# The third chunk's q and k by seven block products, and the gate's logits as two more columns of v

## The chip, the cores and the metric

One core of one Trainium2 chip runs the whole kernel. The metric is device time in microseconds (us): the median of the runs, here 413.5 us over three runs (413.33 to 413.57).

## The reference, cut to what matters

```python
# x: [1, 2048, 448]; 16 heads of 28; window W = 8, dilation 2; F = 1792
g = sigmoid((x * gate_w).sum(-1, keepdims=True))      # one logit per token
qkv = x @ wqkv                                        # [2048, 448] @ [448, 1344]
# attention: each token looks at itself and 7 earlier tokens, 2 apart
logits = einsum("bhsd,bhswd->bhsw", q, kg) * scale    # masked, softmax
a = einsum("bhsw,bhswd->bhsd", attn, vg) ... @ wo
h = relu(x @ w1 + b1); b = (h * h) @ w2 + b2
return g * a + (1 - g) * b
```

All is float32, and the kernel keeps that accuracy with a faster matmul type: each operand is split into a high part (rounded to the type `fp32r`) and a low part (what is left), and a product is the sum of three: high by high, high by low, low by high.

## The kernel before, in words

**Tiles and stages.** The 2048 tokens are four chunks of 512 (`CH`), each four tiles of 128. The contraction over 448 is three full tiles of 128 rows and one of 64. TensorE is used as two halves of 64 rows: two products of 64 rows run side by side, one on the low and one on the high rows, each into its own PSUM bank ("a pair"). A bank that has been added to from one half must not be added to from the other before the first half's work has ended. The kernel sees to that with a *turn*: a one-element memset on VectorE into the bank (`turn`, L196), which TensorE's next product into that bank has to wait for. The written order puts other pairs between a turn and the product that needs it.

Phase A goes through chunks 0, 1, 2 and 3 and computes q, k and v: chunk 0 in `qkv_first`, the others in two calls of `qkv_two`, 63 pairs each (`run`, `side_by_side`). Results go from PSUM to a stage tile by ScalarE (`qkv_evacuate`, L205) and to DRAM (`q_d`, `k_d`, `v_d`, L211). Raw tiles are loaded into a pool of two buffers (`raw_tile`); ScalarE casts the high part (L115), VectorE subtracts for the low part (L116, `split_full`). In chunk 3 a w1 piece's row also goes through one PSUM bank: ScalarE casts and copies it (L514, L515), and VectorE subtracts from the copy (L520, `split_copied`). The bank holds one row at a time.

The gate's logits are worked out on VectorE from the raw x (`z_product`, `z_sums`, L680 to L687), stored to `z_d`, loaded in another layout, and summed (`z_last`).

Phase B is the MLP over the four chunks, with the output products of the attention put between. The attention's own products run on GpSimd (L335, L342), their sums on VectorE (L336, L350). GpSimd begins when the first loads of q, k and v (L306, L307, L312) have come in.

**What sets the order.** Nothing is reordered: each engine runs its instructions as written, and so does SyncE, which issues all DMAs. The writing is driven by a clock of the kernel's own: each pair adds 203 ns (`MM448`) to it in `advance`, and work is put on a list with a due time (`when(time, ...)`, `at(delay, ...)`, `soon` is 1.5 us later). Whenever `advance` is called, all that is due is written in order of its due time, and after it the attention's next pieces; `flush` writes the VectorE reduce of a piece two pieces later. So an operation that is written before a turn stands before it on its engine, whatever it waits for. The table of due times is at L750 to L776, the loop over the chunks at L793 to L806. At the end of chunk 1 the attention is switched on, and its first three loads are written there.

Of the kernel before, what the change touches and what calls it, by code (L numbers as in the profile page):

```python
# [14 lines left out]
P = 128  # L15
# [8 lines left out]
NQ = D + 2  # L24
NZ = 64
NP = 512
# [31 lines left out]
def gated_mix_kernel(ctx: ExitStack, tc: tile.TileContext, xT, wqkv, w1, w2, wo, b1, b2, out):  # L58
# [11 lines left out]
    z_d = tc.dram_tile([P, NZ], F32, name="z_d")  # L70
# [10 lines left out]
    w1h = const.tile([P, 3, F], F32R, name="w1h")  # L81
    w1l = const.tile([P, 3, F], F32R, name="w1l")
# [8 lines left out]

    xpool = ctx.enter_context(tc.tile_pool(name="xpool", bufs=1))
# [5 lines left out]
    zg = smallp.tile([P, 6, NS], F32, name="zg")  # L98
    zt, gt, g1t = zg[:, 0:2], zg[:, 2:4], zg[:, 4:6]
# [54 lines left out]
    wqh = ap.tile([P, 3, NP + 2 * D], F32R, name="wqh")  # L154
    wql = ap.tile([P, 3, NP + 2 * D], F32R, name="wql")

    w7h = ap.tile([P, NP + D], F32R, name="w7h")
    w7l = ap.tile([P, NP + D], F32R, name="w7l")
# [3 lines left out]
    nc.gpsimd.memset(halo0, 0.0)  # L162

    stage = {}

    def block(b):

        o = (0, NP, NP + D)[b]
        return slice(o, o + D)
# [29 lines left out]
    def qkv_evacuate(pt, c, tl, b):  # L199
        par, t = c // 2, (c % 2) * 4 + tl  # L200
        first = (b, t // 2) not in stage
        if first:
            stage[b, t // 2] = xap.tile([P, G, 2, C], F32, tag="stage", name=f"st{c}_{tl}_{b}", bufs=ST_BUFS)
        st = stage[b, t // 2]
        nc.scalar.activation(st[:, :, t % 2], pt[:, :D].rearrange("p (g c) -> p g c", g=G), AF.Copy)  # L205
        if not first:
            stage.pop((b, t // 2))
            t0 = t - t % 2
            dst, off = ((q_d, 0), (k_d, HALO), (v_d, HALO))[b]
            dd = dst[par, :, off:off + SP].rearrange("g (p s) c -> p g s c", s=NS)[:, :, t0:t0 + 2]  # L210
            nc.sync.dma_start(dd.rearrange("p g s c -> p g (s c)"), st.rearrange("p g s c -> p g (s c)"))  # L211
# [9 lines left out]
    def last(x, acc, tl, b):  # L221

        sl = slice(tl * P, tl * P + P)
        n = block(1) if b == 2 else slice(0, D)
        h, l = w7h[:, n], w7l[:, n]
        return [(acc, x.x7[:, sl], h), (acc, x.x7[:, sl], l), (acc, x.x8[:, sl], h)]

    def accs(c, b, tls, tags):
        return [Acc(t, f"qkv{c}_{tl}_{b}", D) for t, tl in zip(tags, tls)]
# [60 lines left out]


# [101 lines left out]
    def gates(par):  # L393

        e = smp.tile([P, 32], F32, tag="e", name=f"e{par}")[:, :NS]
        nc.scalar.activation(e, zt[:, par], AF.Exp, scale=-1.0)
# [127 lines left out]
    def w1_piece(i, dt, gap):  # L524
# [4 lines left out]
        sl = slice(i * n, (i + 1) * n)  # L529

        def part(k):
            if k < 3 and i > 1:
                split_copied(dt + k * gap, raw[:, k, :n], [(slice(0, P), slice(0, n), w1h[:, k, sl], w1l[:, k, sl])])
                return
            if k < 3:
                split_full(raw[:, k, :n], w1h[:, k, sl], w1l[:, k, sl], soon)
# [48 lines left out]
    def h_full(x, acc, f, ks):  # L585
        fs = slice(f * P, f * P + P)
        return sum((three(acc, w1h[:, k, fs], w1l[:, k, fs], x.h[k], x.l[k]) for k in ks), [])
# [11 lines left out]
    def h_turn(accs, f):  # L599
        touch(w1h[:, 2].rearrange("p (f n) -> p f n", n=P)[:, f:f + 2, 0:1])  # L600
# [36 lines left out]
    raws = [raw_tile("wqraw0")]  # L637
    rx = raw_tile("xraw0")
    for k in range(4):
        if k < 3:  # L640
            nc.sync.dma_start(raws[0][:, k, :NQ], wqkv[0, :, k])
        else:
            for b, rows in ((0, slice(0, 64)), (1, slice(64, P))):
                nc.sync.dma_start(raws[0][rows, k, :NQ], wqkv[b, rows, k])
# [3 lines left out]
    for b, tag in ((1, "k"), (2, "v")):  # L648
        raw = attp.tile([P, 3, D], F32, tag=tag, name=f"wqraw{b}")
        for k in range(3):  # L650
            nc.sync.dma_start(raw[:, k], wqkv[b, :, k, :D])
        raws.append(raw)
    raw7 = attp.tile([P, D], F32, tag="q", name="wqraw7")
    nc.sync.dma_start(raw7, wqkv[2, :, 3, :D])
    x = x_tiles(0, xap)
    for k in range(3):
        nc.scalar.activation(wqh[:, k, :D], raws[0][:, k, :D], AF.Copy)
# [7 lines left out]
        nc.vector.tensor_sub(wql[:, k, :D], raws[0][:, k, :D], f32(wqh[:, k, :D]))  # L665
        for cols in halves:
            nc.vector.tensor_sub(x.l[k][:, cols], rx[:, k, cols], f32(x.h[k][:, cols]))
    split_full(raws[0][:, 3, :D], w7h[:, :D], w7l[:, :D])
    split_x78(rx[:, 3], x.x7, x.x8)

    zs = smp.tile([P, 3, NZ], F32, tag="lg", name="zs")
    zu = xcp.tile([P, CH], F32, tag="zu", name="zu")
    zpart, zall, gw = zs[:, 0], zs[:, 1], zs[:, 2, 0:4]
    nc.vector.tensor_copy(gw, raws[0][:, :, D])

    def z_product(raw, k):

        r = slice(0, P if k < 3 else 64)
        if k:
            nc.vector.scalar_tensor_tensor(zu[r], raw[r, k], gw[r, k:k + 1], zu[r], op0=ALU.mult, op1=ALU.add)  # L680
        else:
            nc.vector.tensor_scalar_mul(zu, raw[:, 0], gw[:, 0:1])

    def z_sums(c):

        nc.vector.transpose(zu, zu)
        nc.vector.tensor_reduce(  # L687
            zpart.rearrange("p (b c t) -> p c t b", b=4, c=4)[:, c],
            zu.rearrange("p (t b r) -> p t b r", t=4, b=4), axis=AX.X, op=ALU.add)

    def z_store():

        nc.sync.dma_start(z_d, zpart)

    def z_load():

        for b in range(4):
            nc.sync.dma_start(
# [522 lines left out]
```

## Time and profile before

| | |
|---|---|
| median of three runs | 413.5 us (413.33 to 413.57) |
| span of the profiled execution | 412.0 us |
| TensorE busy | 407.8 us, 99% |
| VectorE / ScalarE / GpSimd busy | 270.6 / 210.4 / 268.4 us |
| granted TensorE clock | 1.000 |
| DMA moved | 73.83 MB, mean 179 GB/s |

The page gives for the profiled execution only its span, from the first to the last instruction; the runs' times hold what lies around it as well. In a line of the timeline the columns are: start, duration, engine, line, operation, what it writes and reads, shape, how many were merged, and in brackets the idle time before it with what ended it. A line of the waits reads: who waited for whom, us in total, how many times, the longest. A line of the DMA issues reads: what was moved, how many times, KB each, median us from issue to landing.

### The profile page before, as it was taken

How to read it: one execution, taken by the hardware profiler on the slowest of the kernel's cores; microseconds unless marked ns; L12 is line 12 of the kernel's file. 1: busy time of each engine (PE TensorE's matmuls, PEld its weight loads, DVE VectorE, ACT ScalarE, POOL GpSimd, SP SyncE). 2: the span in 40 equal slices, each digit the busy share in tenths (PEclk: the TensorE clock that was granted, in tenths of full speed). 3: DMA queues.
4: the chain of work that ended last, by engine and by line, in shares of the span. 5: the costliest groups of instructions: out<-in, count | busy, mean ns of one | idle time of the engine just before them, and what ended most of it. 6: DMA issues, size and time to landing. Idle time of an engine off the chain costs nothing.

```text
span 412.0 us, 9331 instructions
## 1 busy us (share of the span) xinstructions
PE 407.8 (99%) x3835; PEld 366.0 (89%) x3835; DVE 270.6 (66%) x430; ACT 210.4 (51%) x461; POOL 268.4 (65%) x167
## 2 busy tenths in 40 slices
PE   8999999999999999999999999999999999999997
PEld 7999999999888888888888888989898888888996
DVE  4590745276767766787656798879576677892354
ACT  4641646387775555444565535444653254346540
POOL 0000001955999999989989899999899977940000
PEclk9999999999999999999999999999999999999999
DMA  7999999979262315654112649765146530168304
GB/s 213 368 351 309 286 390 288 355 223 315 91 241 99 128 51 209 208 186 152 41 47 105 222 158 270 196 146 154 28 157 200 217 130 2 45 179 132 95 0 181
DMA packets 66763, 73.83 MB, mean 179 GB/s; under 512 B 33120, under 2 KB 59296, under 8 KB 66464
## 3 DMA queue, kind: packets, MB, share of 16 engines
q1 hardware_dynamic: 66720, 73.23, 55.4%
q8 instruction: 30, 0.49, 0.5%
q14 instruction: 13, 0.11, 0.1%
HBM read 45.74 MB, written 28.28 MB: 180 GB/s over the span
## 4 chain that ended last, share of the span: by engine, by line
PE 99%; DVE 0%; issue 0%
PE b L186 33%; PE h L186 32%; PE qkv L186 23%; PE a L186 7%; PE qkv L255 2%; PE warm L634 1%; PE a L993 1%; PE last L993 0%; DVE bt L872 0%; PE last L985 0%; PE a L985 0%; DVE zero L631 0%; DVE b1z L632 0%
## 5 line engine op out<-in xcount | busy, mean ns | idle before, releaser
L335 POOL TENSOR_TENSOR qk<-q,k 128x896 f32<-128x896 f32 x64 | 135.2, 2144 | 84.2 <-DMA k<-k_d 76.0
L342 POOL TENSOR_TENSOR av<-lg,v 128x896 f32<-128x896 f32 x64 | 119.2, 1957 | 6.2 <-DVE lg L336 5.6
L621 DVE TENSOR_TENSOR h<-h,h 128x512 fp32r<-128x512 f32 x56 | 38.4, 688 | 66.8 <-ACT h L624 66.5
L186 PE MATMUL qkv<-wqh,x 64*128 64x448 f32 x528 | 78.2, 359 | 0.0
L336 DVE TENSOR_REDUCE lg<-qk 128x32 f32<-128x896 f32 x64 | 67.0, 1074 | 0.0
L350 DVE TENSOR_REDUCE o<-av 128x112 f32<-128x896 f32 x64 | 66.4, 1070 | 0.1
L186 PE MATMUL b<-w2ah,h 64*128 64x448 f32 x448 | 66.3, 359 | 0.0
L186 PE MATMUL b<-w2bh,h 64*128 64x448 f32 x448 | 66.1, 359 | 0.0
L622 ACT ACTIVATE h<-h,b1z 128x512 f32<-128x512 f32 x56 | 36.7, 655 | 43.6 <-PE h L186 43.6
L186 PEld LDWEIGHTS qkv<-wqh,x 64*128 64x128 f32 x528 | 49.4, 184 | 3.6
L186 PE MATMUL qkv<-wql,x 64*128 64x448 f32 x264 | 47.7, 358 | 0.0
L186 PEld LDWEIGHTS b<-w2bh,h 64*128 64x128 f32 x448 | 42.1, 184 | 3.5
L186 PEld LDWEIGHTS b<-w2ah,h 64*128 64x128 f32 x448 | 42.0, 184 | 3.7
L205 ACT ACTIVATE st<-qkv 128x448 f32<-128x448 f32 x48 | 23.5, 542 | 34.3 <-PE qkv L186 31.7
L186 PE MATMUL b<-w2bl,h 64*128 64x448 f32 x224 | 40.7, 358 | 0.0
L186 PE MATMUL b<-w2al,h 64*128 64x448 f32 x224 | 40.5, 358 | 0.0
L623 ACT ACTIVATE h<-h 128x512 fp32r<-128x512 f32 x56 | 33.5, 598 | 1.7
L624 ACT ACTIVATE h<-h 128x512 f32<-128x512 f32 x56 | 33.3, 594 | 0.0
L573 ACT ACTIVATE h<-h 128x4 fp32r<-128x4 f32 (+1 forms) x35 | 7.2, 207 | 44.4 <-PE b L186 44.2
L186 PE MATMUL h<-x2b,w1h 64*128 64x512 f32 x168 | 28.1, 386 | 0.0
L186 PE MATMUL h<-x,w1h 64*128 64x512 f32 x168 | 28.1, 386 | 0.0
L186 PE MATMUL h<-x1b,w1h 64*128 64x512 f32 x168 | 28.1, 386 | 0.0
(150 smaller groups left out, 688.6 us busy)
## 6 DMA issues: line engine op xcount, KB each, us to landing
k<-k_d SPq DMA_DIRECT2D x8, 840.0 KB, 5.6
v<-v_d SPq DMA_DIRECT2D x8, 840.0 KB, 5.0
x_d<-x SPq DMA_DIRECT2D x11, 512.0 KB, 6.8
q_d<-st SPq DMA_DIRECT2D x8, 448.0 KB, 5.5
k_d<-st SPq DMA_DIRECT2D x8, 448.0 KB, 5.2
v_d<-st SPq DMA_DIRECT2D x8, 448.0 KB, 5.8
w1raw<-w SPq DMA_DIRECT2D x4, 896.0 KB, 9.2
q<-q_d SPq DMA_DIRECT2D x8, 448.0 KB, 3.6
```

The lines of the kernel that those rows point to most:

```text
L186: nc.tensor.matmul(acc.pt[:, :acc.n], a[rows], w[rows], start=acc.todo == acc.all, stop=acc.todo == 1)
L205: nc.scalar.activation(st[:, :, t % 2], pt[:, :D].rearrange("p (g c) -> p g c", g=G), AF.Copy)
L255: nc.tensor.matmul(acc.pt[:, :D], a, w, start=k == j == 0, stop=False)
L335: nc.gpsimd.tensor_mul(pr, q[:, s:s + 1].to_broadcast([P, W, C]), k[:, s:s + W])
L336: pending.append(lambda: nc.vector.tensor_reduce(lg[:, s], pr.rearrange("p w (h d) -> p w h d", h=HG), axis=AX.X, op=ALU.add))
L342: nc.gpsimd.tensor_mul(pr.rearrange("p (h d) w -> p w h d", h=HG), lg[:, s][:, :, :, None].to_broadcast([P, W, HG, DH]), v[:, s:s + W].rea ...
L350: nc.vector.tensor_reduce(o[:, g * C:(g + 1) * C], pr, axis=AX.X, op=ALU.add)
L573: nc.scalar.activation(ap, f32(ap), AF.Copy)
L621: nc.vector.tensor_sub(hl, pt, f32(hh))
L622: ops += [lambda pt=pt, r=r: nc.scalar.activation(pt, pt, AF.Relu, bias=b1t[:, f + r:f + r + 1]), lambda pt=pt, hh=hh: nc.scalar.activatio ...
L623: lambda pt=pt, hh=hh: nc.scalar.activation(hh, pt, AF.Square),
L624: lambda pt=pt, r=r, low=low: (nc.scalar.activation(pt, pt, AF.Square), at(delays[r], low))]
```

## The change

**q and k of chunk 2** are no longer computed tile by tile. Two groups (tiles 0 and 1; tiles 2 and 3) each take q and k of their two tiles as a 2 by 2 block product, cut into halves of the contraction, by seven products of sums instead of eight (Strassen's way). A half is a full tile of 128 and 64 rows more; what is left of the contraction (64 rows) is added in the plain way. For this, sums of weights (`wsum`) are made on VectorE in chunks 0 and 1, in place in the raw weights, and sums of tokens (`sums`) at the end of chunk 1, in place in the raw x of chunk 2. All four sums of `token_sums` are VectorE additions; each result is split into high and low. v of the chunk is written between the products.

A bank takes several of the seven products in turn: its content is copied to a stage tile on ScalarE (`copied`) or added to it on VectorE (`added`), and the next product is added on in the bank.

**The gate's logits** become two more columns of v's weights, 450 instead of 448, in all chunks. ScalarE copies the logit column out of the bank. The code on VectorE and the way through `z_d` go.

**Buffers.** The second half of w1 (`w1b`, six tiles) lies in a pool `halfp` of tags e0 to e5. Before w1 gets there, e0 to e3 hold first the raw q weights and then the token sums, and e4 the k stage of the second group. The raw q weights no longer take a raw buffer. x of chunk 1 has its fourth tile elsewhere, and chunk 3's copies of x (`x_copies`) are made in chunk 3 instead of chunk 2. The stage tiles of v in chunk 2 come from the pool of the attention's products.

**Due times.** Chunk 3's raw x is loaded at 47.5 us of the clock instead of 39.5, the second w1 piece at 54.0 instead of 46.5 with its first cast at 60.5 instead of 58.5; the later pieces are due 1.0 to 2.0 us sooner.

The diff, cut to its core:

```diff
+    def w1_second():
+        for n in range(2):
+            for k in range(3):
+                w1b[n][k] = halfp.tile([P, FA], F32R, tag=f"e{3 * n + k}", name=f"w1b{'hl'[n]}{k}")
...
-    def qkv_evacuate(pt, c, tl, b):
+    def qkv_evacuate(pt, c, tl, b, inner=False):
...
+        nc.scalar.activation(st[:, :, t % 2], heads(pt), AF.Copy)
+        if b == 2:
+            nc.scalar.activation(zt[par][:, t:t + 1], pt[:, D:D + 1], AF.Copy)
...
+    def beside(low, high):
+        assert len(low[1]) == len(high[1])
+        for a in range(0, len(low[1]), 3):
+            for i in range(a, a + 3):
+                for bank, prods in (low, high):
+                    bank.add(*prods[i])
+            advance(3 * MM448)
+
+    def turned(*banks):
+        for bank in banks:
+            nc.vector.memset(bank.pt[0:1, 511:512], 0.0)
...
+    class Group:
...
+        def first(self, n):
+            return self.to(n), sum((passes(*(tuple(v[self.rows] for v in o) for o in self.operands(n, half)))
+                                    for half in (False, True)), [])
+        def second(self, n):
+            return self.to(n), passes(*(tuple(v[self.others] for v in o) for o in self.operands(n, False)))
+        def rest(self, n, r, b):
+            a, w = self.tokens(r, 2), weights(b, 2)
+            return self.to(n), passes(*(tuple(v[self.others] for v in o) for o in (a, w)))
+        def to(self, n):
+            name = {1: "x", 2: "y", 3: "z", 4: "w", 5: "z", 6: "x", 7: "x"}[n]
...
+        def stage(self, b):
+            if self.st[b] is None:
+                if b == self.u == 1:
+                    t = halfp.tile([P, FA], F32, tag="e4", name=f"st{self.c}_{self.u}_{b}")
...
+        def copied(self, n, b, r):
+            nc.scalar.activation(self.stage(b)[:, :, r], heads(self.to(n).pt), AF.Copy)
+        def added(self, n, b, r, store=False):
+            st = self.stage(b)
+            nc.vector.tensor_add(st[:, :, r], heads(self.to(n).pt), st[:, :, r])
+            if store:
+                stage_store(st, self.c // 2, (self.c % 2) * 4 + 2 * self.u, b)
+
+    def qkv_seven(c, x, inner):
+        two = [Group(c, u, x) for u in range(2)]
...
+        v = V(c, x, (0, 1), inner)
+        v.first()
+        first(1)
+        v.second()
+        first(2)
+        second(1)
+        each("copied", 1, 0, 0)
+        first(5)
+        second(2)
+        other(2, 0, 0)
+        each("added", 2, 0, 0)
+        second(5)
+        each("copied", 5, 1, 1)
+        first(6)
+        first(4)
+        second(6)
+        each("copied", 6, 1, 0)
+        other(3, 0, 1)
+        second(3, True)
+        second(4)
+        first(7)
+        other(4, 1, 0)
+        v = V(c, x, (2, 3), inner)
+        v.first()
+        second(7)
+        each("copied", 7, 0, 1)
+        each("added", 4, 0, 1, True)
+        first(3, False)
+        each("added", 3, 1, 0)
+        v.second()
+        other(7, 1, 1)
+        each("added", 7, 1, 1, True)
...
     def h_turn(accs, f):
-        touch(w1h[:, 2].rearrange("p (f n) -> p f n", n=P)[:, f:f + 2, 0:1])
+        if f == NFA - 1:
+            for r in range(2):
+                touch(w1_f(0, 2, f + r)[:, 0:1])
+        else:
+            half = w1_rows(0, 2)[f // NFA].rearrange("p (f n) -> p f n", n=P)
+            touch(half[:, f % NFA:f % NFA + 2, 0:1])
...
+    def weight_sums():
+        (q0, q1, q2, m), (k0, k1, k2) = ([t[:, :D] for t in raws[b]] for b in range(2))
+        o = raw7[:, 1, :D]
+        sub = nc.vector.tensor_sub
+        def cut(key, t):
+            return lambda: split_full(t, *wsum[key], soon)
+        def by_halves(low, high):
+            return [lambda: low(LOW), lambda: high(HIGH)]
+        return [lambda: split_full(o, *w7x, soon),
+                lambda: sub(q0, k0, q0), lambda: sub(k0, k1, k0), cut((1, False), q0),
+                lambda: sub(k1, k1, q0), cut((3, False), k0), lambda: sub(q1, q1, k1),
+                cut((2, False), k1), cut((4, False), q1),
+                lambda: sub(q2, k2, q2),
+                *by_halves(lambda r: sub(k2[r], o[r], k2[r]), lambda r: sub(k2[r], m[r], k2[r])),
+                cut((1, True), q2), cut((3, True), k2),
+                *by_halves(lambda r: sub(o[r], o[r], q2[r]), lambda r: sub(m[r], m[r], q2[r])),
+                *by_halves(lambda r: sub(m[r], m[r], o[r]), lambda r: sub(o[r], o[r], m[r])),
+                *by_halves(lambda r: split_full(o[r], *(t[r] for t in wsum[2, True]), soon),
+                           lambda r: split_full(m[r], *(t[r] for t in wsum[2, True]), soon)),
+                *by_halves(lambda r: split_full(m[r], *(t[r] for t in wsum[4, True]), soon),
+                           lambda r: split_full(o[r], *(t[r] for t in wsum[4, True]), soon))]
+
+    def token_sums(c):
...
+        def cut(j):
+            split_full(xraw[c][:, j], *(t[:, :CH] for t in sums[c, j]), soon)
+            for u, rows in enumerate((LOW, HIGH)):
+                split_full(xraw[c][rows, 2 + j, u * 2 * P:(u + 1) * 2 * P], *(t[rows, CH:] for t in sums[c, j]), soon)
+        return [lambda: add(r(two, 1), r(two, 1), r(one, 1)), lambda: sub(r(one, 1), r(one, 0), r(one, 1)),
+                lambda: sub(r(one, 0), r(two, 1), r(one, 0)), lambda: sub(r(two, 0), r(two, 0), r(one, 0)),
+                lambda: (begin(), cut(1)), lambda: cut(0)]
...
-        xm[c] = x_tiles(c, xpool)
-        xs[c] = X(own + xm[c].t[3:])
-        for j in range(3):
-            at(12000.0 + j * 2000.0, lambda j=j: nc.scalar.activation(xm[c].t[j], f32(own[j]), AF.Copy))
+        xs[c] = X(own + [xpool.tile([P, 2, CH], F32R, tag="x3", name=f"x{c}_3")])
+
+    def x_copies(c):
+        own = xs[c].t
+        xm[c] = X([xpool.tile([P, 2, CH], F32R, tag=f"x{j}", name=f"x{c}_{j}") for j in range(3)] + own[3:])
+        for j in range(3):
+            at(3000.0 + j * 2000.0, lambda j=j: nc.scalar.activation(xm[c].t[j], f32(own[j]), AF.Copy))
...
-    SPLIT_AT = {1: 19000.0, 2: 35000.0, 3: 53500.0}
+    SPLIT_AT = {1: 19000.0, 2: 35000.0, 3: 55000.0}
...
+    steps(17000.0, 900.0, weight_sums())
...
-            when(t + 4500.0, x_more, c + 1)
...
+    when(23500.0, x_more, 2)
+    when(47500.0, x_more, 3)
+    when(46900.0, lambda: steps(47000.0, 900.0, token_sums(2)))
...
-    when(46500.0, w1_piece, 1, 58500.0, 1500.0)
-    when(67000.0, w1_piece, 2, 77400.0, 1450.0)
-    when(68000.0, w1_piece, 3, 83300.0, 1450.0)
-    when(70000.0, biases)
-    when(86000.0, w2_piece, 0, 4, 93000.0, 1400.0)
-    when(89600.0, w2_piece, 4, 3, 100200.0, 1400.0)
+    when(54000.0, w1_piece, 1, 60500.0, 1500.0)
+    when(66000.0, w1_piece, 2, 75600.0, 1450.0)
+    when(67500.0, w1_piece, 3, 81500.0, 1450.0)
+    when(68000.0, biases)
+    when(84000.0, w2_piece, 0, 4, 91200.0, 1400.0)
+    when(87600.0, w2_piece, 4, 3, 98400.0, 1400.0)
...
+    qkv_first(xs[0])
+    qkv_two(xs[1], 1, 0)
+    qkv_two(xs[1], 1, 2)
+    st_["spilled"] = 0
+    clock["on"] = True
+    clock["att"] = clock["pe"] - 1.0
+    advance(0.0)
+    qkv_seven(2, xs[2], True)
+    x_copies(3)
+    x = xs[3]
+    qkv_two(x, 3, 0, copies=True)
+    qkv_two(x, 3, 2, (mlp_one, mlp_two), True)
+    st_["spilled"] = 1
```

More of the change, by code (lines that the diff above doesn't have):

```diff
@@ L228, in accs @@
     def accs(c, b, tls, tags):
[L229 removed]
+        return [Acc(t, f"qkv{c}_{tl}_{b}", NV if b == 2 else D) for t, tl in zip(tags, tls)]
     def run(c, todo, steps):
@@ L585, in h_full @@
     def h_full(x, acc, f, ks):
-        fs = slice(f * P, f * P + P)
-        return sum((three(acc, w1h[:, k, fs], w1l[:, k, fs], x.h[k], x.l[k]) for k in ks), [])
+        return sum((three(acc, w1_f(0, k, f), w1_f(1, k, f), x.h[k], x.l[k]) for k in ks), [])
     def h_last(x, acc, f):
@@ L722, in x_begin, with steps @@
+    def steps(t, gap, fns):
+        for i, fn in enumerate(fns):
+            when(t + i * gap, fn)
     def x_begin(c):
```

240 lines of the change are left out of this document (151 added, 89 removed).

## The prediction

> **What bounds the kernel now.** I read the page first, then TensorE's row of the timeline, then SyncE's, ScalarE's and VectorE's rows between 46 and 93 us, then the waits.
>
> ```profile
> span 412.0 us, 9331 instructions
> PE 407.8 (99%) x3835; PEld 366.0 (89%) x3835; DVE 270.6 (66%) x430; ACT 210.4 (51%) x461; POOL 268.4 (65%) x167
> ...
> PE 99%; DVE 0%; issue 0%
> ```
>
> TensorE is busy for 407.8 of 412.0 us and is the whole chain that ended last. So a matmul taken out is time gained, and a wait that TensorE has not got today is time lost; no other engine gives any of it back. The span stands 1.5 us under the median of 413.5 us; I sum on the median.
>
> ```profile
> 52.66 0.56 PE L186 MATMUL qkv<-wqh,x 64*128 64x448 f32 x4
> ...
> 56.26 0.56 PE L186 MATMUL qkv<-wqh,x 64*128 64x448 f32 x4
> ...
> 104.60 0.40 PE L186 MATMUL h<-x,w17h 64*128 64x512 f32 x2
> ...
> 107.37 0.36 PE L186 MATMUL qkv<-wqh,x 64*128 64x448 f32 x2
> ```
>
> These are starts. 52.66 to 56.26 holds 18 pairs of 64-row products, 0.200 us a pair of 448 columns; the twelve pairs of 512 columns of the MLP's first visit take 104.60 to 107.37, 0.231 us each, so a column is 0.5 ns. The pair at 56.26 is the last of chunk 1, and chunk 2 begins at 56.46. The kernel's own clock (203 ns a pair) says 51.16 there, since 252 pairs lie behind it; that lets me turn its due times into places among the pairs.
>
> **The gain.** q and k of a chunk are 4 x 2 x 21 = 168 products, 84 pairs. In the new order each of two groups has seven times 6 + 3 products and four times 3, 75 in all, beside the other group: 75 pairs. Nine pairs are gone: 9 x 0.200 = 1.80 us. The gate's two columns ride on 168 pairs of v: 168 x 2 x 0.5 ns = 0.17 us. **Net -1.63 us.** The Z work (16 multiply-adds, 4 transposes, 4 sums) leaves VectorE, and 22 steps of weight sums come to it in about the same stretch, chunks 0 and 1; at 0.6 to 0.7 us a step they replace what goes (rows below), so I take nothing for them, with a bound of 0.5 us if a turn there is late.
>
> **What is queued behind what.** A turn is a memset on VectorE that TensorE must wait for before the other rows may add into a bank. VectorE runs it in written order, behind everything written ahead.
>
> ```profile
> 46.95 0.34 SPq L567 DMA_DIRECT2D xraw<-xT  x1
> 47.34 2.63 SPq L142 DMA_DIRECT2D x_d<-x  x4
> ...
> 52.49 0.59 SPq L528 DMA_DIRECT2D w1raw<-w  x1
> 55.43 0.38 SPq L211 DMA_DIRECT2D q_d<-st  x1
> 55.91 0.47 SPq L211 DMA_DIRECT2D k_d<-st  x1
> 57.72 0.85 SPq L211 DMA_DIRECT2D v_d<-st  x1
> 63.16 0.33 SPq L306 DMA_DIRECT2D q<-q_d  x1
> 64.51 0.34 SPq L307 DMA_DIRECT2D k<-k_d  x1
> 65.85 0.32 SPq L312 DMA_DIRECT2D v<-v_d  x1
> ```
>
> ```profile
> SPq L306 <- DMA q_d<-st: 4.5, 1, 4.5
> ```
>
> ```profile
> 56.71 0.98 ACT L205 ACTIVATE st<-qkv 128x448 f32<-128x448 f32 x2 [0.87 <-ACT st L205]
> 57.72 2.19 ACT L115 ACTIVATE x<-xraw 128x512 fp32r<-128x512 f32 x4
> 61.87 1.05 ACT L115 ACTIVATE w1h<-w1raw 128x448 fp32r<-128x448 f32 x2 [1.96 <-DMA w1raw<-w]
> 70.48 2.95 ACT L736 ACTIVATE x<-x 128x1024 fp32r<-128x1024 f32 x3
> ```
>
> ```profile
> k<-k_d SPq DMA_DIRECT2D x8, 840.0 KB, 5.6
> v<-v_d SPq DMA_DIRECT2D x8, 840.0 KB, 5.0
> ...
> q_d<-st SPq DMA_DIRECT2D x8, 448.0 KB, 5.5
> k_d<-st SPq DMA_DIRECT2D x8, 448.0 KB, 5.2
> ...
> w1raw<-w SPq DMA_DIRECT2D x4, 896.0 KB, 9.2
> ```
>
> ```profile
> DMA to landing us min/median/max: 6.4/9.2/9.7
> ```
>
> SyncE stands still until chunk 1's stores land (4.5 us for q), then issues the attention's three loads at 63.16, 64.51 and 65.85, one per landed store: 1.3 us for 448 KB in queue order, 345 KB/us. The second w1 piece, issued at 52.49, came in at 61.87, when ScalarE had waited 1.96 us for it; the last row is the landing of such pieces, 6.4 to 9.7 us.
>
> **First loss: that w1 piece.** It moves from 46.5 to 54.0 on the clock, so from ahead of the attention's loads (written at 51.16) to behind them. With its 896 KB out of the way the stores land 896/345 = 2.6 us sooner, v's at 63.2 instead of 65.85; only then can SyncE issue v's load and, at about 63.5, w1. Ahead of it lie 448 + 840 + 840 KB of loads: by queue order 63.2 + (448 + 840 + 840 + 896)/345 = 72.0; by the shortest and longest landing 69.9 and 73.2. I take **71.5**, near queue order, as transfers overlap at the seams. Its first cast is due at 60.5, after pair 48 of chunk 2; the low part, 1.5 later, is written after pair 57, just ahead of the turn of bank x after product 6. TensorE needs that turn for pair 64, at 56.46 + 63 x 0.2 + 0.4 (next part) = 69.5. It gets it at landing + cast 0.6 + subtract 0.6 + memset 0.1 = landing + 1.3 = 72.8: **3.3 us** lost (1.7 to 5.0). Today the same cast waits too, but the turns lie elsewhere and the wait is hidden.
>
> **The short turns** earlier in chunk 2. Between v's first part and its second lie only 6 pairs, 1.2 us, and ScalarE still has the token sums to cast: 0.1. Between product 2's parts lie 15 pairs' worth from v's end, 3.0 us, in which v's two copies (0.98), two gate columns, x3's last two casts (2.19 for four, so 1.1), the subtract (0.69) and the memset must pass, 3.3 in all: 0.3. Together **0.4**, bounds 0 and 1.0. The next chunk's raw x, now loaded at 53 rather than 46.95, comes behind the spill and ahead of the stores, at about 59; ScalarE gets to its first cast at 59 to 60 (the copies that end at 57.7 today, and 1.3 us of casts for each of two token sums, worked out from the four casts in 2.19), and anything up to 61 hides behind the wait for v.
>
> ```profile
> 58.38 0.69 DVE L116 TENSOR_TENSOR x<-xraw,x 128x512 fp32r<-128x512 f32 x1 [5.91 <-DMA v_d<-halo]
> ...
> 83.83 0.62 DVE L520 TENSOR_TENSOR w1l<-copy,w1h 128x448 fp32r<-128x448 f32 x1 [5.06 <-ACT copy L515]
> ...
> 87.13 1.08 DVE L336 TENSOR_REDUCE lg<-qk 128x32 f32<-128x896 f32 x1
> 88.20 0.06 DVE L196 MEMSET qkv<- 1x1 f32 x2
> 88.32 1.13 DVE L520 TENSOR_TENSOR w17l<-copy,w17h 64x128 fp32r<-64x128 f32 x4
> 89.37 1.07 DVE L336 TENSOR_REDUCE lg<-qk 128x32 f32<-128x896 f32 x1
> 90.38 0.64 DVE L520 TENSOR_TENSOR w1l<-copy,w1h 128x448 fp32r<-128x448 f32 x1
> 90.44 0.06 DVE L196 MEMSET qkv<- 1x1 f32 x2
> ```
>
> ```profile
> 86.58 1.22 ACT L514 ACTIVATE w17h<-w1raw 64x128 fp32r<-64x128 f32 x4
> 87.71 0.53 ACT L515 ACTIVATE copy<-w1raw 128x448 f32<-128x448 f32 x1
> ```
>
> **Second loss: chunk 3's first two turns.** Today chunk 3 starts at 56.46 + 25.2 = 81.66. The turns at 88.20 and 90.44 stand before pairs 37 and 46, at 88.86 and 90.66: 0.6 and 0.2 us to spare. In front of them go, in turn, ScalarE's cast and copy of a w1 row into the one copy bank and VectorE's subtract from it. Two things now enter that chain. (a) The low row k=1 of w1's second half goes into the half-buffer e4, which holds the k stage of the second group; that group's last add ends about 1.5 us into chunk 3 (two adds of 0.62 behind the last pair), and the store is issued at 1.9. Transfers to and from k's buffer land so:
>
> ```profile
> DMA to landing us min/median/max: 3.8/5.8/8.6
> ```
>
> Between 3.8 and 5.8 (the page has 5.2 for the stores alone) I take 4.5, since the queue is emptier by then: 6.4. The subtract is written at 78.35 and stands at the head of VectorE until then; behind it are two reduces (79.66 now falls ahead of the turn, like 77.36) and the turn: 6.4 + 0.6 + 2.1 = 9.1 against pair 37 at 7.2: 1.9 us (1.3 to 3.3; nothing if the store were no matter, since then the turn stands at 6.5). (b) x3's three copies (2.95 us in chunk 2 today) fall due 3, 5 and 7 us into chunk 3, one of them in front of the four w17 casts, and the subtract of row k=2 is due at 79.80 while the turn is written at 79.78, so it slips behind the turn. From that turn: subtract 0.6, copy 0.55, four subtracts 1.13, reduce 1.07, memset: 3.4 us, where 9 pairs give 1.8: 1.6 more (1.1 without (a)). **Together 3.5 us**, 1.1 to 4.9.
>
> **Sum:** 413.5 - 1.63 + 0.4 + 3.3 + 3.5 = **419.1 us**. The 16 gate copies, the doubled touch per chunk and the eight adds of chunk 2 lie on engines with a third or more of their time free and ahead of no turn I have not counted; if one were, 0.2 to 0.6 us each.
>
> **Rivals.**
> 1. *Faster.* All turns come in time: the w1 piece lands by 68.2 and the e4 store does not hold VectorE, nor do x3's copies. 413.5 - 1.63 + 0.4 = 412.3. It decides at those two moments. For it: a landing of 6.4 is on record, and VectorE is only 66% busy. Against it: SyncE's order, and 0.2 us to spare today.
> 2. *Only chunk 2 waits* (the e4 store lands early and the copies fit): 412.3 + 3.3 = 415.6.
> 3. *Only chunk 3 waits* (w1 lands early): 412.3 + 3.5 = 415.8.
> 4. *TensorE loses its clock.* After a stop as long as the 3.3 us of chunk 2, the next matmuls run slow, as at the start:
>
> ```profile
> 1.19 3.14 PE L634 MATMUL warm<-zero 128*128 128x256 f32 x13 [1.19 <-DVE b1z L632]
> ```
>
> Thirteen of 256 columns in 3.14 us is 0.94 ns a column, half the rate of the 0.200 us pairs; a stretch as long costs 1.6 us: 420.7. The Trainium skill, "TensorE: Matmul & The Clock Gate", Part 1, has such a rule: after at least one idle window of about 3.4 us the clock is halved until a busy window has passed. By it a stop under 3.4 us costs nothing more and one well over it costs this; the slow start here agrees, and no row of this trace shows a stop later on.
>
> **How the numbers follow.** Forecast (both waits) 0.45; rival 1 0.15; rival 2 0.16; rival 3 0.13; rival 4 0.11. A change under 0.2% (0.8 us) can't be told from none. Faster takes rival 1 less a tail of it, 0.13; no change 0.06, a mild form of rivals 1 to 3; slower 0.81. The range leaves out rival 1 and the upper end of rival 4: 414.0 to 421.8; the forecast's own is 417 to 421.5.
>
> **What would show it.** Right: an idle TensorE of 2 to 5 us about 69 us into the span, ended by VectorE's memset, with ScalarE waiting for w1raw; w1raw issued after the attention's v load; two idle stretches of TensorE in the first half of chunk 3, the first with VectorE waiting for the k_d store; 18 fewer matmuls. Wrong: a TensorE without idle time between 56 and 95 us, a w1 landing before 68, or a low part of w1 that does not stand ahead of the turn.

## The result, and the profile after

The changed kernel takes **434.42 us** (median of four runs, 434.18 to 436.27), the kernel before 413.41 us on the same chip: 1.051 times as long (95% interval 1.049 to 1.054). Forecast were 419.1 us, in a range of 414.0 to 421.8. The side was right, and the loss is nearly four times what was forecast: 21 us instead of 5.6.

The page of the changed kernel, its first lines and the shares of the chain that ended last:

```profile
span 434.4 us, 9353 instructions
PE 413.8 (95%) x3817; PEld 396.7 (91%) x3817; DVE 278.6 (64%) x450; ACT 220.0 (51%) x498; POOL 267.4 (62%) x167
...
PE 83%; DMA 7%; ACT 4%; DVE 2%; POOL 1%; issue 1%; SPq 0%; POOLq 0%; DVEq 0%; ACTq 0%
```

Eighteen matmuls are gone (3835 to 3817), as the change says. But TensorE is no longer the whole chain: 83% instead of 99%, the rest being DMAs and the engines behind them. And though it has 18 matmuls less, it is busy for 6.0 us more (413.8 against 407.8), which is a sign that some of them ran slowly. The profiled execution is the longest of the four; the other three have spans of 432.4 to 432.7.

What TensorE waited for, from its waits (us in total, times, longest):

```profile
PE x L334 <- DVE x L350: 5.9, 1, 5.9
PE qkv L201 <- DVE qkv L211: 4.6, 2, 3.2
PE h L201 <- ACT w1ah L794: 2.6, 1, 2.6
PE h L201 <- ACT st L233: 1.9, 1, 1.9
```

The first is chunk 2's stop, the second both of chunk 3's. The last two lie in the second half of chunk 3, and no step of the prediction has them.

**Where the time went.** The first pair of chunk 3 and the first product into bank b, from TensorE's rows of the changed kernel:

```profile
90.40 0.36 PE L201 MATMUL qkv<-wqh,x 64*128 64x448 f32 x2
...
137.18 0.36 PE L201 MATMUL b<-w2ah,h 64*128 64x448 f32 x1
```

Before, chunk 3 began at 81.66 and the first b product stood at 116.57. So chunk 2 (with 0.1 of chunk 1) cost 8.7 us, chunk 3 with the MLP's first visit 11.9 us. Behind it the profiled execution loses 1.8 us more, 1.2 of it up to the last matmul. This goes with the attention's late loads (below): in the traces of experiments 1 to 3, which have them too, this stretch is 1.1 us longer than before, in that of experiment 4, where they are repaired, 0.2.

**Chunk 2.** SyncE's queue, ScalarE's wait, VectorE's rows, and TensorE around the stop:

```profile
61.27 0.33 SPq L523 DMA_DIRECT2D q<-q_d  x1
63.28 0.33 SPq L524 DMA_DIRECT2D k<-k_d  x1
64.72 0.32 SPq L529 DMA_DIRECT2D v<-v_d  x1
65.09 0.61 SPq L745 DMA_DIRECT2D w1raw<-w  x1
```

```profile
75.29 0.58 ACT L129 ACTIVATE w1ah<-w1raw 128x448 fp32r<-128x448 f32 x1 [9.13 <-DMA w1raw<-w]
```

```profile
75.90 0.63 DVE L130 TENSOR_TENSOR w1al<-w1raw,w1ah 128x448 fp32r<-128x448 f32 x1 [6.93 <-ACT w1ah L129]
76.52 0.06 DVE L350 MEMSET x<- 1x1 f32 x2
```

```profile
69.95 0.77 PE L334 MATMUL w<-tw,x 64*128 64x448 f32 x6
76.66 0.74 PE L334 MATMUL x<-w2ah,s_0h 64*128 64x448 f32 x2 [5.94 <-DVE x L350]
77.19 0.58 PE L334 MATMUL x<-w2al,s_0h 64*128 64x448 f32 x2
...
82.05 0.56 PE L334 MATMUL x<-w2ah,s_0l 64*128 64x448 f32 x2
82.42 0.39 PE L334 MATMUL x<-w2ah,s_0h 64*128 64x448 f32 x2
```

The order is the predicted one: w1 is issued behind v's load and lands 10.2 us later, and the cast, the subtract and the memset of bank x's turn follow in a row. What comes next was only a rival: from 76.66 to 82.42 lie 15 pairs in 5.76 us, 0.37 us a pair and more, where they take 3.0 at 0.200. The windows of TensorE (stretch, length, busy, granted clock, DMA share, GB/s) say why:

```profile
72.00:76.00 4.00, 0.00 (x0) 0.95 1.05 383
76.00:80.00 4.00, 3.34 (x18) 0.50 0.14 50
80.00:84.00 4.00, 4.00 (x32) 0.69 0.17 31
```

The granted clock is 0.50 behind the stop. That is 2.8 us.

**Chunk 3, first half.** VectorE's wait at the head of its queue:

```profile
98.32 0.62 DVE L737 TENSOR_TENSOR w1bl<-copy,w1bh 128x448 fp32r<-128x448 f32 x1 [4.62 <-DMA k_d<-st]
```

The row that goes into e4 waits until 98.32, 7.9 us into the chunk, for the store of k. TensorE stops for 3.24 us (until 101.06) and 1.31 us (until 104.46).

**Chunk 3, second half.** SyncE's rows of the changed kernel, and of the kernel before for the same two loads:

```profile
102.19 0.37 SPq L777 DMA_DIRECT2D w2raw<-w  x1
109.94 0.36 SPq L225 DMA_DIRECT2D q_d<-st  x1
110.39 0.46 SPq L225 DMA_DIRECT2D k_d<-st  x1
110.90 0.90 SPq L777 DMA_DIRECT2D w2raw<-w  x1
111.89 1.21 SPq L523 DMA_DIRECT2D q<-q_d  x1
113.16 0.47 SPq L524 DMA_DIRECT2D k<-k_d  x1
```

```profile
90.46 0.34 SPq L306 DMA_DIRECT2D q<-q_d  x1
90.85 0.42 SPq L307 DMA_DIRECT2D k<-k_d  x1
```

The attention's second loads used to go out ahead of chunk 3's first stores (95.69 before). Now they stand behind these and behind w2's second piece, and go out 21 to 22 us later, though chunk 3 itself begins only 8.7 us later. GpSimd, VectorE and ScalarE, in this order, show what hangs on them:

```profile
120.68 6.23 POOL L552 TENSOR_TENSOR qk<-q,k 128x896 f32<-128x896 f32 x3 [16.50 <-DMA k<-k_d]
```

```profile
122.83 1.09 DVE L553 TENSOR_REDUCE lg<-qk 128x32 f32<-128x896 f32 x1 [5.54 <-POOL qk L552]
123.84 0.61 DVE L737 TENSOR_TENSOR w2al<-copy,w2ah 128x448 fp32r<-128x448 f32 x1
```

```profile
124.49 0.55 ACT L732 ACTIVATE copy<-w2raw 128x448 f32<-128x448 f32 x1 [4.56 <-DVE w2al L737]
124.97 0.19 ACT L794 ACTIVATE w1ah<-w1ah 128x2 fp32r<-128x2 f32 x1
```

VectorE waits at a reduce for GpSimd's late product; behind it stands the subtract that empties the copy bank; ScalarE waits for that, and behind ScalarE's copy stands the touch that releases the MLP's next product. TensorE stops until 125.21 (2.57 us) and again until 129.66 (1.88 us), and its clock is down a second time: 0.78 and 0.79 in the windows 128 to 132 and 132 to 136.

### The profile page after: what moved, and what is told of

The parts are those of the page before. It is cut to its first block, busy times and chain, and to the rows that moved or that the text cites. A ratio compares the mean times of both kernels' runs of the same rounds, so it can differ in the third digit from the quotient of the medians.

```text
span 434.4 us, 9353 instructions
## 1 busy us (share of the span) xinstructions
PE 413.8 (95%) x3817; PEld 396.7 (91%) x3817; DVE 278.6 (64%) x450; ACT 220.0 (51%) x498; POOL 267.4 (62%) x167
## 4 chain that ended last, share of the span: by engine, by line
PE 83%; DMA 7%; ACT 4%; DVE 2%; POOL 1%; issue 1%; SPq 0%; POOLq 0%; DVEq 0%; ACTq 0%
PE b L201 30%; PE h L201 29%; PE qkv L201 10%; PE a L201 7%; DMA w1raw<-w 2%; PE qkv L281 2%; DMA k<-k_d 2%; POOL qk L552 1%; DMA k_d<-st 1%; DMA q_d<-st 1%; PE v L334 1%; ACT st L233 1%; ACT copy L732 1%; PE x L334 1%; PE z L334 1%
## 5 line engine op out<-in xcount | busy, mean ns | idle before, releaser
L201 PE MATMUL b<-w2ah,h 64*128 64x448 f32 x448 | 75.0, 359 | 0.0
L201 PE MATMUL qkv<-wqh,x 64*128 64x448 f32 (+1 forms) x384 | 61.6, 362 | 4.6 <-DVE qkv L211 4.6
L201 PEld LDWEIGHTS b<-w2ah,h 64*128 64x128 f32 x448 | 59.8, 184 | 0.3
L201 PEld LDWEIGHTS b<-w2bh,h 64*128 64x128 f32 x448 | 56.4, 184 | 1.6 <-DVE h L846 0.7
L201 PE MATMUL b<-w2al,h 64*128 64x448 f32 x224 | 55.8, 358 | 0.0
L201 PE MATMUL b<-w2bl,h 64*128 64x448 f32 x224 | 53.2, 359 | 0.0
L201 PE MATMUL qkv<-wql,x 64*128 64x448 f32 (+1 forms) x192 | 45.7, 361 | 0.0
L201 PEld LDWEIGHTS b<-w2al,h 64*128 64x128 f32 x224 | 35.0, 184 | 0.1
L201 PEld LDWEIGHTS b<-w2bl,h 64*128 64x128 f32 x224 | 32.7, 184 | 0.4
L201 PEld LDWEIGHTS qkv<-wql,x 64*128 64x128 f32 x192 | 26.2, 185 | 0.7
```

Of the source, the lines that this page charges most:

```text
L201: nc.tensor.matmul(acc.pt[:, :acc.n], a[rows], w[rows], start=acc.todo == acc.all, stop=acc.todo == 1)
```

## The experiments

**1. w1 ahead of the attention.** The attention is switched on 3.3 us later by the kernel's clock, with as much taken off its later delay, so that its three loads stand behind the w1 piece in SyncE's queue.

```diff
-ATT_DELAY = 17000.0
+ATT_DELAY = 13700.0
-    clock["att"] = clock["pe"] - 1.0
+    clock["att"] = clock["pe"] - 1.0 + 3300.0
```

> The changed kernel (434.4 us), with the attention's first three loads written 3.3 us of the kernel's clock later, so that the second w1 piece stands ahead of them in SyncE's order; the attention's pieces keep their due times. Theory (SyncE's order makes w1 late, VectorE's order hands it to TensorE): w1raw is issued at about 61 us, as soon as its buffer is free, and lands at 68 to 70; the stop of 5.9 us after product 4 falls under 1.5 us, and the stretch at half clock behind it (3.3 us) goes too: 425 to 428 us. Rival 1 (the DMA queues are full, so w1 is late in any order): it lands after 73, stop over 3 us, 431 to 434. Rival 2 (six pairs are too few for a turn, whatever w1 does): the stop stays at 5 to 6 us, 434.

Measured: 428.99 us (one run), 1 us above the range expected. w1 is issued at 60.52 and the stop at bank x's turn after product 6 is gone; the granted clock is 1.00 through chunk 2. A stop of 0.65 us stays at 77.56: VectorE's third subtract of the piece takes 2.18 us and the last four 4.74, while GpSimd multiplies from 69.86 on (experiments 5 to 7 take this up). But chunk 3's first stop is now longer, and the half clock stands behind that one. TensorE's row and windows:

```profile
93.79 0.74 PE L201 MATMUL qkv<-wqh,x 64*128 64x448 f32 x2 [4.48 <-DVE qkv L211]
```

```profile
92.00:96.00 4.00, 2.21 (x12) 0.54 0.02 4
96.00:100.00 4.00, 4.00 (x28) 0.60 0.69 227
```

So the w1 piece is the cause of the first stop; and once it is repaired, TensorE reaches chunk 3 8.5 us sooner and waits there for k's store again: VectorE's row stands until 91.05, 9.2 us into the chunk.

**2. k's stage moved.** The second group's k stage lies in another buffer (tag x2), so that w1's row needn't wait for its store.

```diff
-                    t = halfp.tile([P, FA], F32, tag="e4", name=f"st{self.c}_{self.u}_{b}")
-                    self.st[b] = t.rearrange("p (g s c) -> p g s c", g=G, s=2)
+                    t = xpool.tile([P, 2, CH], F32, tag="x2", name=f"st{self.c}_{self.u}_{b}")
+                    self.st[b] = t.rearrange("p a n -> p (a n)")[:, :FA].rearrange("p (g s c) -> p g s c", g=G, s=2)
```

> The changed kernel, with the second group's k stage in a tile of x's copies (tag x2) instead of half-buffer e4. Theory (VectorE waits for the k_d store to be read out of e4): VectorE's wait of 4.6 us for k_d goes, the first stop of chunk 3 (3.4 us) goes with it, the second (1.5) stays within 1 us; 430 to 432 us. Rival (the two reduces and the copies in front of the turn hold it, the store only fills the gap): the first stop stays over 2 us, 433 to 435.

Measured: 431.27 us (one run). Of chunk 3's two stops only 0.47 us is left (at 99.72); x3's copies stand where they stood. So the e4 store made nearly all of both stops, and the copies of x3 half a microsecond at most. The rest is as in the changed kernel (6.9 us at w1, the half clock, the two late stops).

**3. TensorE kept busy through the wait.** Eighteen pairs whose result is thrown away are put ahead of the product that waits.

```diff
+        for i in range(FILL):   # 18
+            for bank, rows in zip(v.banks, (LOW, HIGH)):
+                nc.tensor.matmul(bank.pt[:, :NV], x.h[0][rows, 0:P], weights(2, 0)[0][rows], start=True, stop=True,
+                                 skip_group_check=True)
         second(6)
```

> The changed kernel with 18 pairs of products that nobody reads (3.7 us of TensorE at full clock) written between product 4 and the second part of product 6, into the banks that v takes next. Clock theory: the wait for w1 ends when it ended (76.6 us), but TensorE is busy for 3.7 of the 5.9 us and its pairs behind it take 0.20 us instead of 0.37: 3.3 us less, 431 us. Rival (the slow pairs come from something else than the pause, such as loads that use the same memory): the pairs stay slow, 434 to 438 us.

Measured: 429.81 us (one run). The w1 piece is as late as before, and the stop behind the fill is 1.96 us. The windows after it:

```profile
76.00:80.00 4.00, 3.85 (x38) 1.00 0.07 26
80.00:84.00 4.00, 4.00 (x44) 1.00 0.72 224
```

The clock stays at 1.00 with more work done: the half clock comes from the idle time. In the trace chunk 2 takes 30.5 us instead of 33.8; 2.8 of these 3.3 us are the clock, the rest is that the wait ends at 76.15 instead of 76.66. The gain of 4.6 us by the medians is larger, since chunk 3 is shorter too: its first stop is 1.76 us instead of 3.24, and the last late one 0.48 instead of 1.88.

**4. The attention's second loads ahead again.** The changed kernel with one number changed: the attention's first products are planned 1.85 us sooner.

```diff
-ATT_DELAY = 17000.0
+ATT_DELAY = 15150.0
```

> The changed kernel (434.42 us) with the attention's first products planned 1.85 us sooner and nothing else; the second unit's loads then stand ahead of the fourth chunk's stores and of w2's second piece on SyncE again, as in the kernel before. Theory A (the two late stops of 2.6 and 1.9 near 125 to 130 and the half clock behind them come from that order): both vanish with the half clock, the loads go out near 103 instead of 112, and the time is 434.4 - 5.9 = 428.5 us (427.5 to 429.5); the stops of 5.9 near 76 and of 3.2 and 1.3 near 101 to 104 stay. Theory B (they are only a consequence of the earlier delays: w2's first piece goes out at 102 anyway): they stay, 434.

Measured: **428.4 us** (428.28 to 428.8, four runs). The loads stand behind w2's first piece and ahead of the stores again:

```profile
102.49 0.37 SPq L777 DMA_DIRECT2D w2raw<-w  x1
102.95 0.46 SPq L523 DMA_DIRECT2D q<-q_d  x1
103.46 0.42 SPq L524 DMA_DIRECT2D k<-k_d  x1
110.24 0.37 SPq L225 DMA_DIRECT2D q_d<-st  x1
```

They go out at 102.95 and 103.46 instead of 111.89 and 113.16, both late stops are gone, and TensorE is busy all through 120 to 136 at a clock of 1.00. The stops of chunk 2 (6.81) and chunk 3 (2.25 and 2.31) stay. That of chunk 2 is 0.9 us longer than before this edit, though w1's first subtract begins sooner (75.33 against 75.90): two subtracts take 4.21 us there, while GpSimd multiplies from 70.48 to 79.06. So this one number is worth 6.0 us, though w2's first piece goes out at 102.5 as before. It moves all of the attention's pieces by 1.85 us, not the two loads alone; that the late stops hang on the loads is read from the rows of the section before.

**5. All three repairs.** Experiments 1, 2 and 4 together, x3's copies 10 us later, and the casts of w1's third piece 0.1 us sooner.

```diff
-ATT_DELAY = 17000.0
+ATT_DELAY = 11850.0
-    clock["att"] = clock["pe"] - 1.0
+    clock["att"] = clock["pe"] - 1.0 + 3300.0
# k's stage in tag x2, as in experiment 2
-            at(3000.0 + j * 2000.0, lambda j=j: nc.scalar.activation(xm[c].t[j], f32(own[j]), AF.Copy))
+            at(13000.0 + j * 2000.0, lambda j=j: nc.scalar.activation(xm[c].t[j], f32(own[j]), AF.Copy))
-    when(66000.0, w1_piece, 2, 75600.0, 1450.0)
+    when(66000.0, w1_piece, 2, 75500.0, 1450.0)
```

> The changed kernel with all: w1 ahead of the attention's loads, the k stage out of e4, x's three copies due 13, 15 and 17 us into chunk 3 instead of 3, 5 and 7, the attention's pieces 1.85 us sooner (so that they fall among chunk 3's pairs as before the change), w1's third piece 0.1 us sooner (so that its third low row stands ahead of the first turn). Theory (the 22 us are waits in written order and their clock, and the nine pairs are a gain): no stop over 1 us, 412 to 414 us, at or under the 413.4 of before. Rival (the seven products with their adds are themselves too much for VectorE and ScalarE): stops of 2 us and more remain in chunk 2 and 3, 416 to 422 us.

Measured: 417.75 us (416.62 to 420.44, four runs). A miss: slower than expected, and 1.012 times the kernel before (1.009 to 1.016). Beside two short stops of 0.3 a stop of 2.42 us stands at 79.53, for a turn at which VectorE came late. VectorE's and GpSimd's rows:

```profile
69.68 0.62 DVE L130 TENSOR_TENSOR w1al<-w1raw,w1ah 128x448 fp32r<-128x448 f32 x1 [0.21 <-ACT w1ah L129]
...
70.59 2.20 DVE L130 TENSOR_TENSOR w1al<-w1raw,w1ah 128x448 fp32r<-128x448 f32 x1
...
72.91 6.48 DVE L130 TENSOR_TENSOR w17l<-w1raw,w17h 64x64 fp32r<-64x64 f32 x4
```

```profile
70.18 8.75 POOL L552 TENSOR_TENSOR qk<-q,k 128x896 f32<-128x896 f32 x4 [68.79 <-DMA k<-k_d]
```

A subtract of the same kind and size takes 0.62 us before GpSimd begins and 2.20 just after. Was GpSimd the cause, or something else that began then?

**6. The subtracts first.** w1's subtracts are written sooner, and the attention's first loads another 2.7 us later, so that the subtracts are done before GpSimd begins.

```diff
-ATT_DELAY = 11850.0
+ATT_DELAY = 9150.0
-    clock["att"] = clock["pe"] - 1.0 + 3300.0
+    clock["att"] = clock["pe"] - 1.0 + 6000.0
-            when(dt + k * gap, part, k)
+            when(gap[k] if i == 1 else dt + k * gap, part, k)
-    when(54000.0, w1_piece, 1, 60500.0, 1500.0)
+    when(54000.0, w1_piece, 1, 0.0, (60500.0, 61000.0, 61500.0, 63400.0))   # one due time per row
```

> Against the kernel with all three repairs (417.75 us, a stop of 2.42 at 79.53): the four subtractions of w1's second piece are put earlier (all done by about 72) and the attention's first loads 2.7 us later, behind v's first store, so that GpSimd starts near 73. Theory A: that stop comes from VectorE's subtractions from SBUF running 2.2 and four in 6.5 us instead of 0.6 and 1.2 while GpSimd multiplies; then here they take 0.62 each and 1.2 for four, the stop at 79.5 is gone, the span is 414.9 - 2.42 - 0.1 = 412.4 and the time 414.1 us (413.6 to 414.6). Theory B: the subtractions are slow for another reason (the landing of the piece, a DMA beside them): they stay at 2 us and the time stays at 416 to 418. No stop over 0.5 us is expected but the two short ones of product 1 and 2 (0.3 each).

Measured: **413.85 us** (413.15 to 414.17, eleven runs), 1.0005 times the kernel before (0.9995 to 1.0016); the profiled span is 412.3, forecast was 412.4. The four subtracts take 1.17 us (70.56 to 71.7), GpSimd begins at 71.77, and of TensorE's stops only 0.32 and the like of the short turns are left.

**7. The same loads, the subtracts left where they were** (experiment 5 with the attention's two numbers of experiment 6).

> As the kernel with all three repairs, with the attention's first loads 2.7 us later only; the subtractions of w1's second piece stay where they were (the first three near 68.7 to 71.2, the last four from 72.9). Theory A (GpSimd beside them slows them): GpSimd starts near 73, the third takes 0.62 instead of 2.20, the four last run beside GpSimd's first product and take 1.2 to 4 instead of 6.5; the stop of 2.42 shrinks to 0 to 0.5 and the time is 414 to 415. Theory B (another reason): 2.2 and 6.5 us again, 417.

Measured: 419.08 us median, 413.85 to 420.26 over ten runs. The execution with a trace (414.02 us) had what was expected, but seven of the ten were 4 to 6 us longer, which no theory had put down. The same kernel ran twice more with a trace:

> The kernel with the attention's loads 2.7 us later and w1's subtractions left where they were, once more: its ten executions lay between 413.85 and 420.26 us, and the one with a trace was one of the short ones (the four last subtractions took 1.24 us in all and ended at 73.7, GpSimd began at 73.64). Theory A: in a long execution (418 to 420) GpSimd's first product begins before these four, near 72, they take 4 to 6.5 us, and TensorE stops for 2 to 5 us behind them near 77 to 80. Theory B: the long ones have another cause; the four take 1.2 us in them too.

> The same kernel again, for a second trace: by theory A the length of the four last subtractions of w1's second piece (1.2 us, or 4 to 6.5) goes with the time (414, or 418 to 420); by theory B it does not.

They took 420.14 and 419.14 us. VectorE's and GpSimd's rows, first of the short execution, then of the one of 420.14:

```profile
72.49 1.24 DVE L130 TENSOR_TENSOR w17l<-w1raw,w17h 64x64 fp32r<-64x64 f32 x4
...
73.64 10.46 POOL L552 TENSOR_TENSOR qk<-q,k 128x896 f32<-128x896 f32 x5 [72.25 <-DMA k<-k_d]
```

```profile
72.23 8.28 DVE L130 TENSOR_TENSOR w17l<-w1raw,w17h 64x64 fp32r<-64x64 f32 x4
...
71.98 8.38 POOL L552 TENSOR_TENSOR qk<-q,k 128x896 f32<-128x896 f32 x4 [70.59 <-DMA k<-k_d]
```

In the execution of 419.14 the four took 8.16 us, with GpSimd from 71.76. It is one kernel: whether GpSimd begins 0.25 us before the subtracts or 1.2 us after their start decides over 7 us of VectorE. In the trace of 420.14 each of the four ends 0.08 to 0.15 us after one of GpSimd's products (at 74.20, 76.34, 78.44 and 80.52, the products at 74.12, 76.20, 78.29 and 80.37). The loads beside them are not the cause: the last two run in a window in which the DMAs moved 3 GB/s (76 to 80, below), while in experiment 6 subtracts ran undelayed where they moved 377 GB/s (68 to 72). A stop of 3.74 us follows (3.62 in the other), and the half clock behind it. TensorE's windows of the execution of 420.14:

```profile
76.00:80.00 4.00, 0.91 (x10) 0.89 0.01 3
80.00:84.00 4.00, 3.35 (x18) 0.50 0.44 134
84.00:88.00 4.00, 4.00 (x34) 0.75 1.07 371
```

**8. The memsets of the two short turns first.** Experiment 6, and on VectorE v's and y's turns stand ahead of the subtracts that held them up.

```diff
-            when(t + i * gap, fn)
+            when(52200.0 if t == 47000.0 and i == 5 else t + i * gap, fn)   # the last token sum
-            when(t + k * 900.0, lambda c, k: x_split(xraw[c], xs[c], k), c, k)
+            when((55000.0, 55900.0, 57900.0, 57950.0)[k] if c == 3 else t + k * 900.0, lambda c, k: x_split(xraw[c], xs[c], k), c, k)
```

> As the run before, and on VectorE the memsets of the turns of v's and y's banks stand ahead of the subtractions that held them up (three of the token sums, two of the fourth chunk's x). Theory A (the two short stops are these subtractions): both stops of 0.3 vanish, with about 0.1 of refilling behind each, 0.8 in all, and the time is 413.3 us, that is equal to the kernel before within 0.2. Theory B (they are the turn itself: the memset has to wait for the last pair's end and TensorE for the memset): stops of about 0.3 stay, 414.1.

Measured: 413.06 us (412.56 to 415.26, twelve runs), 0.9995 times the kernel before (0.9982 to 1.0009). No stop of TensorE is left but the one at the very start, so the short stops were these subtracts and not the turn as such. It is the best form of the change found, 0.35 us under the kernel before by the medians, and that can't be told from no change.

## Why the prediction was wrong, and where it was right

The forecast was 419.1 us and is 15.3 us short. Two steps of it failed. It let the second w1 piece land at 71.5, where it landed at 75.27; that made the first stop 5.94 us instead of 3.3 and brought the half clock, 2.8 us, which stood in the sum at nothing. And it put down nothing for the second half of chunk 3, where the attention's second loads, now behind chunk 3's stores in SyncE's queue, cost 6.0 us. The mechanism, waits by written order, was right all through, and both predicted waits came where they were put.

**The gain (-1.63 us)** came in its place, a little smaller, and holds only in part to the end. In experiment 8, without a stop, chunk 2 takes 23.8 us (56.4 to 80.17) against 25.2, 1.4 us less where nine pairs are 1.8; the first b product stands 1.23 us sooner than before (115.34 against 116.57), the last matmul 1.03 us sooner (407.68 against 408.71), and the median 0.35. What is lost of it lies partly in v's pairs of 450 columns, of which rows show some at 0.207 us and some at 0.200; the 0.17 us forecast for the gate's columns was too little or something else adds to it, and that stays open.

**The short turns (0.4 us)** were right in kind and place. TensorE stands for 0.32 us at v's second part, and at product 2's two starts lie 0.28 us further apart than a pair takes. Experiment 8 shows the queue named for them as the cause: chunk 2 takes 23.81 us there and 24.54 in experiment 6, so they are worth 0.7 us, within the bounds of 0 and 1.0.

**The first loss** was right in its mechanism, and mis-sized: 3.3 forecast, 5.94 measured. The term that failed is the landing. The step took 63.5 for the issue and 71.5 for the landing, near queue order, out of 69.9 to 73.2; it was issued at 65.09 and landed at 75.27, after 10.2 us, longer than the longest landing on record before (9.7). The 3.8 us between 71.5 and 75.27 can be read so. v's store, which v's load waits for, landed at 64.7 instead of 63.2 (1.5 us): the prediction took w1's 896 KB out of the stores' way, but not into account the 1024 KB of raw x that the change issues ahead of them, at 54.40. From there to w1's landing the queue took 10.6 us for the 3024 KB that the prediction counts, at most 286 KB/us, where it had used 345, a rate read from stores alone (1.8 us). The other 0.5 is that 71.5 was taken where its own queue order gave 72.0. No run takes these three apart. Issued at 60.5 in experiment 6, ahead of the loads, the same piece came in time.

**Rival 4, the clock,** got a chance of 0.11, since the stop that it was to follow was put at 3.3 us, just under the window of the rule cited beside it. With 5.9 us of stop it came, and its price of 1.6 was too low: 15 pairs in 5.76 us, 2.8 us lost. The mis-sized first loss thus counted twice.

**The second loss** was right in its mechanism: 3.5 forecast, 4.55 measured. Of its parts (a), the e4 store, was put too low (1.9) and (b), x3's copies and the slipped subtract, too high (1.6): with the store out of the way 0.47 us is left. The store landed so that the row stood at 98.32, 7.9 us into the chunk, where 6.4 was forecast. That the sum of the two parts came within 1.1 us of the measured one is partly luck, since their errors lie on opposite sides.

**What the prediction had not: the second half of chunk 3**, 6.0 us by experiment 4. Two things of the change meet there. Nine pairs fewer take 1.8 us off the kernel's own clock ahead of all that chunk 3 writes, and w2's second piece is due at 87.6 instead of 89.6; the attention's pieces keep their distance from the start of chunk 2. So its second loads, written ahead of chunk 3's stores before, are now written behind them and behind w2. Which of the two counts for more was not taken apart; 1.85 us on the attention alone undoes it. The prediction followed the first loads through SyncE's queue and stopped there. It turned the clock into places among the pairs for the work that the change moves, and did not ask what the shorter clock does to the work that keeps its time. Its sentence that the added copies and adds lie ahead of no uncounted turn was beside the point: a load slipped, and the wait went from GpSimd through VectorE and ScalarE to TensorE.

By the terms: -1.0 (the pairs less the gate's columns, to the last matmul of experiment 8) + 0.7 (short turns) + 5.9 (w1) + 2.8 (clock) + 4.6 (chunk 3) + 6.0 (late loads) = 19.0 us of the 21.0 between the medians. The restarts behind the stops are part of the other 2.0 (at product 2's turn 0.28 us are lost between the starts, of which the profile counts 0.11 as idle); the rest is not shown.

## What to carry to other kernels

A step that moves in a written order is to be followed through every queue that it passes, to the end of the stage and not to the first wait it makes: here 1.85 us in one planned delay were worth 6.0 us. Taking work out also moves all that is timed by it against all that is not. Where TensorE runs at 99%, a stop must be priced with the clock behind it, and a landing by what else will be on the queues then, not by landings of before. And a gain of 1.6 us in a chunk with its turns less than 1 us ahead of their use is spent by a single late memset; the repairs that brought the kernel back to even were all a matter of what stands in front of the memset, or of ScalarE's touch, that TensorE waits for.

## What the runs showed of the hardware

**VectorE's subtracts from SBUF stand still while GpSimd multiplies.** A subtract with both inputs in SBUF takes 0.62 us alone and 2.20 beside GpSimd's products, each 2.1 us long (experiment 5); four small ones take 1.2 us alone and 8.28 when GpSimd has begun just ahead of them, one product for each (experiment 7). Adds and subtracts with an input in PSUM show nothing of it: in the changed kernel the subtract from the copy bank at 123.84 takes 0.61 us while GpSimd works from 120.68 on, and in the execution of 420.14 an add from PSUM at 87.67 takes 0.63 us beside a product of 86.65 to 88.78. The Trainium skill, "SBUF — State Buffer", Who interferes with whom, states this rule: a VectorE instruction with two SBUF inputs contends with a GpSimd instruction that reads SBUF, and whichever issues second is blocked until the first is done. The trace agrees, with these numbers. In the kernel before, the rows lay 0.85 us apart: its last subtracts of the kind ended at 70.04 and GpSimd began at 70.89.

**Half the clock after a stop, but not by the stop's length alone.** Stops of 3.62, 3.74, 4.48, 5.94, 6.81 and 6.89 us were followed by a granted clock of about 0.5 for 3 to 6 us; stops of 2.25, 2.31, 2.42 and 3.24 were not. But one of 2.57 us was (experiment 3, in the second half of chunk 3, 0.43 us a pair of 512 columns until 123.5), and in the changed kernel one of 1.88 that followed one of 2.57 at a distance of 2.6 us. The Trainium skill, "TensorE: Matmul & The Clock Gate", Part 1, has a free-running window of about 3.4 us that must be idle; a stop of 2.57 us can't hold such a window whole, so by these rows less than a whole idle window can do it. What fits all the traces is the share of one step. Their records of the granted clock show the half clock in stretches of 3.41, 6.83 or 10.24 us, one, two or three steps of 3.41. Where each trace is cut into such steps, reckoned from the start of its half clock, every step at full clock (from 10 us on) in which TensorE stood idle for 1.88 us or more by the profile is followed by the half clock (1.88, 1.89, 1.92, 1.94, 2.21, 2.24, 3.04, and three of 3.39 to 3.41), and none with less is (1.87, 1.79, 1.70, 1.67 and below). So the stop of 3.24 us cost no clock because it fell across two steps, 1.70 and 1.54 us. It is a reading of these ten cases; no run was made to test it.
